# A fused linear-attention and gated-MLP kernel: one x slab at a time in the key loop, two subtractions in halves, and three conversions moved

## The chip, the cores and the metric

The kernel runs on one core of a Trainium2 chip. The metric is the device time of one launch in microseconds; three runs of the kernel before gave 660.51, 662.21 and 662.61, median 662.21. Engines are named as the profile names them: PE is TensorE (matmuls; PEld is its weight load), DVE is VectorE, ACT is ScalarE, POOL is GpSimd, SP is SyncE, which only issues DMAs here. Each engine works through its own instructions in order and waits on semaphores for the others.

## The reference, cut to what matters

With S = 2048 tokens, D = 640, 32 heads of 20 and F = 1536:

```python
xn = layernorm(x)                                   # over D, eps 1e-5
q, k, v = split(xn @ wqkv)                          # 32 heads of 20
pq, pk = q @ w_phi, k @ w_phi                       # per head, 20 x 20
phi_q = concat(softmax(pq), softmax(-pq))           # 40 features a head
phi_k = concat(softmax(pk), softmax(-pk))
kv, z = phi_k.T @ v, phi_k.sum(tokens)
s = ((phi_q @ kv) / (phi_q @ z + 1e-6)) @ wo
g = silu(gelu(xn @ w1 + b1) @ w2 + b2)
out = x + s * g
```

## The kernel before

All matmuls keep fp32 accuracy by splitting each operand into a high part (a rounded copy, made by ScalarE) and a low part (operand minus high part, made by VectorE or GpSimd) and adding three products: high by high, high by low, low by high (PASSES).

**Phase 1** works on 16 tiles of 128 tokens. A key tile takes `project(t, wk_s)` (30 matmuls into one of three PSUM banks, `bankA`), then the features: `feat1` on VectorE (L382 maximum per head, L385 subtract it and write the slab e, L388 minimum), with a last step on GpSimd (L389, below "rest"), `feat2` on ScalarE (L398, exp in place), and `key_fin` (L406 and L438: sums per head and reciprocals on VectorE, L411: scaling on GpSimd). L385 is what frees the bank. `value(t)` is a second projection whose bank ScalarE empties (L427). `kv_pair` adds two tiles into the key-value state. Query tiles take `project`, `feat1` and `store_e`: exp on ScalarE and the store of e to DRAM from ScalarE's queue.

The **normalized and transposed x** is what the projections read as stationary operand. It is held for two tiles together, called a pair q, in the buffers xp (eight blocks, four pairs at a time) and b12 (a slab for two pairs). For q of 4 to 7 these steps make it from x transposed in DRAM:

- `load_xr(q)`: two DMAs on SyncE's queue (L266, L267) into a slab xr
- `pair_stats`: mean and 1/std of two token tiles (L230 to L235 on VectorE, L233 on GpSimd), written to DRAM and read back as rows bc over all partitions (L331, L333)
- `pair_sub(q)`: minus the mean, on GpSimd (L339); `pair_mul(q)`: times 1/std, on VectorE (L344)
- `pair_plain(q)`: high parts on ScalarE (L285, three instructions), low parts on VectorE (L287, three)
- `t_sums(q)`: five differences on GpSimd (L300), in place in xr
- `t_split(q)`: the same split of the differences into the buffer xd: ScalarE (L321) and GpSimd (L322). It is the last reader of the slab xr.

Before xp's blocks of an old pair are written over, `spill(q)` copies them to DRAM (L295, L296, SyncE).

**Slabs.** One pool of 23 buffers of 5 KB a partition (tag "S") holds the split weights (five each for keys, values and queries), b12, xr, every e, and the forms below. A new tile waits for the last user of the buffer that it gets; where none is free, the engine that writes it waits.

The loop over t = 6 to 9 does for each t a key tile, a value tile and two query tiles (of tiles 0 to 7), and beside them pair work. After it, p = 5, 6, 7 take two key tiles each and then `value_pair(p)`: both value tiles of a pair in seven block products instead of eight (`token_pair`, parts X, Y, X, V, Z, W, Z in the order of QPARTS, numbered 0 to 6). It needs five weights split in halves and three sums of weights, S2, S3 (in the slabs f[0] and f[1]), S1 (in the right halves of wv_s[0], wv_s[1]) and S4 (f[2]). `forms` loads the sums and splits them, one group at each `next`. After part 0, ScalarE copies bank X (L654) before part 2 goes on accumulating in it. `hooks` run behind the numbered parts: hook 1 `rest`, hook 4 `first_key` (`key_fin` of the first key tile), hook 6 `second_key`.

From p = 7 on, four token pairs of queries and twelve units of the MLP follow, and the output projection at the end.

All of this part stands under a manual schedule: every engine takes its instructions in the order of the Python text, which is therefore the order in each queue. In the loop that is

```python
es[t] = feat1(pk)
if t > 6: pair_plain(q - 1)          # q = t - 2
if t < 9: pair_sub(q)
if t < 8: load_xr(q + 1)
feat2(es[t]); vs[t] = value(t); phis[t] = key_fin(es.pop(t))
pq = project(next(queries), wq_s); ef = feat1(pq)
if t > 6: t_sums(q - 1)
if t < 9: pair_mul(q)
```

so that slabs of two or three pairs are in use at a time.

Of the kernel before, what the change touches and what calls it, by code (L numbers as in the profile page):

```python
# [8 lines left out]
F32 = mybir.dt.float32  # L9
# [6 lines left out]
P = 128  # L16
# [30 lines left out]
def hedgehog_gated_mlp_kernel(ctx: ExitStack, tc: tile.TileContext, x, xt_in, wqk, bd, wv, wo, w1, b1, w2, b2, out_t):  # L47
# [270 lines left out]
    def t_split(q):  # L318
        dst = xd()[:, :, :, at(q)]
        tt = xrs.pop(q).rearrange("p k (o t) -> p (k o) t", o=2)[:, :9]  # L320
        nc.scalar.activation(dst[:, :, 0, :], tt, AF.Copy)  # L321
        nc.gpsimd.tensor_tensor(dst[:, :, 1, :], tt, dst[:, :, 0, :].bitcast(F32), op=OP.subtract)  # L322

    def pair_stats(t):
        if t % 2 == 0:
# [9 lines left out]
            pld[q] = bc  # L335

    def pair_sub(q):
        bc, xr = pld.pop(q), xrs[q]
        nc.gpsimd.tensor_tensor(xr, xr, bc[:, None, :, 0].to_broadcast([P, KC, W2]), op=OP.subtract)  # L339
        pld[q] = bc  # L340

    def pair_mul(q):
        bc, xr = pld.pop(q), xrs[q]
# [2 lines left out]
    def pair_plain(q):  # L346
        for o in range(2):
            plain(q, o, xrs[q][:, :, o * P:(o + 1) * P])
# [107 lines left out]
    def kv_pair(t):  # L456
        for u in (t, t + 1):
            kv_acc(u, phis.pop(u), vs.pop(u))
# [146 lines left out]
    def split_to(dst, src, eng):  # L605
        nc.scalar.activation(dst[:, 0], src, AF.Copy)
        eng.tensor_tensor(dst[:, 1], src, dst[:, 0].bitcast(F32), op=OP.subtract)

    def forms(dram, f, base, engs):
        raws = [load_raw(dram[k]) for k in range(4)]  # L610
        yield
        for k in range(4):
            if k < 3:
                f.append(slab(F32R, "ws"))
            if k < 2:
                split_to(f[k][:], raws[k][:], engs[k])
            else:
                split_to(base[k - 2][:, :, HALF:], raws[k][:, HALF:], engs[k])
                split_to(f[2][:, :, (k - 2) * HALF:(k - 1) * HALF], raws[k][:, :HALF], engs[k])
            yield  # L620

    QPARTS = (("X", "A11", 0, None), ("Y", "S2", 10, None), ("X", "A12", 2, ("A1k", 4)), ("V", "S3", 12, ("A2k", 7)),
# [73 lines left out]
    x_in(10)  # L696
    x_in(11)
    for t in range(6, 10):
        q = t - 2
        pk = project(t, wk_s)  # L700
        if t == 8:
            kv_pair(6)
        if t == 9:
            vb = forms(sv_dram, wv_f, wv_s, [nc.vector] * 4)
            next(vb)
            w_dump(0)
            w_dump(1)
        if t == 6:
            next(vf[1])
            spill(3)  # L710
        es[t] = feat1(pk)
        if t > 6:
            pair_plain(q - 1)
        if t < 9:
            pair_sub(q)
        if t == 6:
            fold_w(wqT, range(4, KC), "wq", wq_s)
        if t < 8:
            load_xr(q + 1)
        feat2(es[t])  # L720
        vs[t] = value(t)
        phis[t] = key_fin(es.pop(t))
        pq = project(next(queries), wq_s)
        ef = feat1(pq)
        if t > 6:
            t_sums(q - 1)
        if t < 9:
            pair_mul(q)
        for u in STATS.get(t, ()):
            pair_stats(u)  # L730
        store_e(queries_done.pop(0), ef)
        pq = project(next(queries), wq_s)
        ef = feat1(pq)
        if t == 6:
            next(vf[1])
        if t == 9:
            next(vb)
            next(vb)
        if t > 6:
            t_split(q - 1)  # L740
        store_e(queries_done.pop(0), ef)
        if t == 6:
            kv_pair(4)
        for u in XIN.get(t, ()):
            x_in(u)
    qf, later, last_sums = None, [], []
    for p in range(5, 8):
        t = 2 * p
        pk = project(t, wk_s)
        if p == 7:  # L750
            w1r = load_w1(0)
            qf = forms(sq_dram, wq_f, wq_b, [nc.vector, nc.vector, nc.vector, nc.gpsimd])
            next(qf)
        es[t] = feat1(pk)
        if p == 5:
            load_xr(7)
            next(vb)
        if p == 6:
            pair_mul(7)
        pk = project(t + 1, wk_s)  # L760
        kv_pair(t - 2)
        es[t + 1] = feat1(pk, later)
        if p == 7:
            next(qf)
            next(qf)
            q_back(0)
            q_back(1)
            wq_b.extend(wq_s[2:])
        if p == 6:
            pair_plain(7)  # L770

        def rest(t=t, p=p):
            later.pop(0)()
            feat2(es[t])
            if p == 6:
                t_sums(7)
            if p == 7:
                next(qf)

        def first_key(t=t, p=p):  # L780
            phis[t] = key_fin(es.pop(t))
            feat2(es[t + 1])

        def second_key(t=t, p=p):
            if p < 7:
                phis[t + 1] = key_fin(es.pop(t + 1))
            else:
                phis[t + 1] = es.pop(t + 1)
                last_sums.append(key_sums(phis[t + 1]))
            if p == 5:  # L790
                pair_sub(7)
            if p == 6:
                t_split(7)

        value_pair(p, {0: lambda: p == 5 and next(vb), 1: rest, 2: lambda: p == 7 and next(qf), 4: first_key, 6: second_key})
    w1f = w1_forms(w1r)

    def early_rest(q, ea):
# [522 lines left out]
```

## Time and profile before

| | us |
|---|---|
| median of three runs | 662.21 |
| the profiled execution | 661.99 |
| its span in the trace | 660.3 |
| busy: PE, DVE, POOL, ACT | 649.2, 493.0, 399.2, 237.6 |
| granted TensorE clock, mean of the span | 0.996 |

A timeline row gives start, duration, engine, line and operation, output from inputs, shapes, count, and in brackets how long the engine had been idle before it and what ended that. A row with a count covers neighbours that were merged. Matmuls overlap in the array, so the duration of one row of matmuls reaches a little into the next; distances between starts are the better measure. A row of stretches gives the stretch, its length, the busy time and count of each engine, the granted clock (1.00 is full), the DMA engines' busy share and GB/s. The rows themselves are shown where they are used.

### The profile page before, as it was taken

How to read it: one execution, taken by the hardware profiler on the slowest of the kernel's cores; microseconds unless marked ns; L12 is line 12 of the kernel's file. 1: busy time of each engine (PE TensorE's matmuls, PEld its weight loads, DVE VectorE, ACT ScalarE, POOL GpSimd, SP SyncE). 2: the span in 40 equal slices, each digit the busy share in tenths (PEclk: the TensorE clock that was granted, in tenths of full speed). 3: DMA queues.
4: the chain of work that ended last, by engine and by line, in shares of the span. 5: the costliest groups of instructions: out<-in, count | busy, mean ns of one | idle time of the engine just before them, and what ended most of it. 6: DMA issues, size and time to landing. Idle time of an engine off the chain costs nothing.

```text
span 660.3 us, 11417 instructions
## 1 busy us (share of the span) xinstructions
PE 649.2 (98%) x4396; PEld 562.6 (85%) x4396; DVE 493.0 (75%) x739; ACT 237.6 (36%) x345; POOL 399.2 (60%) x357
## 2 busy tenths in 40 slices
PE   9999999989899999999999999999999999999997
PEld 9999999989889998888888888888888887766866
DVE  5785977597887778768979968859789899853232
ACT  3512322324434256252442444841332424132130
POOL 2755476887677854857778876363472967343321
PEclk9999999999999999999999999999999999999999
DMA  9706299427411287527889699787779399999942
GB/s 351 271 1 174 84 336 248 111 94 220 156 42 41 80 258 270 192 85 274 217 263 318 165 406 324 118 308 256 150 213 243 88 268 207 307 256 259 289 165 79
DMA packets 164447, 135.15 MB, mean 205 GB/s; under 512 B 89394, under 2 KB 128562, under 8 KB 164010
## 3 DMA queue, kind: packets, MB, share of 16 engines
q1 hardware_dynamic: 161658, 122.84, 64.0%
q10 hardware_dynamic: 2736, 11.60, 4.9%
q8 instruction: 34, 0.56, 0.4%
q14 instruction: 19, 0.16, 0.1%
HBM read 86.03 MB, written 48.38 MB: 204 GB/s over the span
## 4 chain that ended last, share of the span: by engine, by line
PE 84%; DVE 6%; POOL 5%; ACT 1%; issue 1%; DMA 1%; SPq 0%; ACTq 0%; DVEq 0%; POOLq 0%
PE pB L907 24%; PE pB L878 21%; PE pA L370 14%; PE pB L1065 11%; PE pA L650 5%; PE pA L174 2%; PE pB L1012 2%; POOL e L389 2%; POOL e L411 1%; POOL xr L300 1%; DVE xp L287 1%; PE qV L650 1%; PE kv L450 1%; ACT e L398 1%; DVE rc L406 1%
## 5 line engine op out<-in xcount | busy, mean ns | idle before, releaser
L907 PE MATMUL pB<-hs,w2s 128*128 128x512 f32 x720 | 165.7, 389 | 0.0
L907 PEld LDWEIGHTS pB<-hs,w2s 128*128 128x128 f32 x720 | 135.0, 188 | 28.8 <-DVE y L916 0.8
L878 PE MATMUL pB<-xp,w1s 128*128 128x512 f32 x324 | 81.4, 389 | 0.2 <-DVE pB L1146 0.2
L878 PE MATMUL pB<-xd,w1s 128*128 128x512 f32 x324 | 79.3, 389 | 0.0
L1065 PE MATMUL pB<-oT,wo 128*128 128x512 f32 (+1 forms) x315 | 72.3, 381 | 0.0
L878 PEld LDWEIGHTS pB<-xp,w1s 128*128 128x128 f32 x324 | 60.7, 188 | 13.2 <-DVE pB L1146 0.7
L878 PEld LDWEIGHTS pB<-xd,w1s 128*128 128x128 f32 x324 | 60.8, 188 | 12.6
L411 POOL TENSOR_TENSOR eq<-eq,rc 128x1280 f32<-128x1280 f32 x16 | 37.9, 2369 | 54.7 <-DVE rc L969 36.7
L1065 PEld LDWEIGHTS pB<-oT,wo 128*128 128x128 f32 x315 | 57.2, 188 | 13.8 <-PE pB L1012 2.5
L916 DVE TENSOR_TENSOR y<-pB,y 128x512 f32<-128x512 f32 x100 | 63.1, 675 | 1.4 <-PE pB L907 1.4
L398 ACT ACTIVATE e<-e 128x1280 f32<-128x1280 f32 x32 | 40.7, 1273 | 60.7 <-POOL e L389 60.7
L389 POOL TENSOR_TENSOR e<-nr,e 128x640 f32<-128x640 f32 x32 | 46.7, 1460 | 22.6 <-DVE nr L388 20.3
L883 ACT ACTIVATE pB<-pB,b1t 128x512 f32<-128x512 f32 x48 | 31.8, 662 | 78.8 <-DVE pB L1146 29.2
L411 POOL TENSOR_TENSOR e<-e,rc 128x1280 f32<-128x1280 f32 x16 | 39.2, 2450 | 34.5 <-DVE rc L438 34.5
L370 PE MATMUL pA<-wk,xp 128*128 128x320 f32 x384 | 59.6, 310 | 0.0
L370 PEld LDWEIGHTS pA<-wk,xp 128*128 128x128 f32 x384 | 56.9, 188 | 0.1
L956 POOL TENSOR_TENSOR ez<-eq,zrep 128x1280 f32<-128x1280 f32 x16 | 47.4, 2961 | 2.6 <-DMA eq<-e_dram 2.6
L478 POOL TENSOR_TENSOR w1s<-raw,w1s 128x640 fp32r<-128x640 f32 (+1 forms) x18 | 25.0, 1391 | 29.4 <-ACT w1s L477 23.3
L370 PE MATMUL pA<-wv,xp 128*128 128x320 f32 x240 | 37.7, 311 | 0.0
L1068 POOL TENSOR_TENSOR xres<-gt,xres 128x256 f32<-128x256 f32 x20 | 14.3, 735 | 35.3 <-DVE gt L1067 35.3
L370 PEld LDWEIGHTS pA<-wv,xp 128*128 128x128 f32 x240 | 35.5, 188 | 0.1
L889 DVE TENSOR_TENSOR hs<-pB,hs 128x512 fp32r<-128x512 f32 x48 | 32.0, 683 | 3.8 <-ACT hs L885 3.6
(182 smaller groups left out, 1148.8 us busy)
## 6 DMA issues: line engine op xcount, KB each, us to landing
raw<-in_w_dram SPq DMA_DIRECT2D x42, 320.0 KB
e_dram<-e ACTq DMA_DIRECT2D x16, 640.0 KB
eq<-e_dram SPq DMA_DIRECT2D x16, 640.0 KB
phi_t<-eq SPq DMA_DIRECT2D x64, 160.0 KB
phT<-phi_t SPq DMA_DIRECT2D x20, 480.0 KB
xt<-in_x_dram SPq DMA_DIRECT2D x16, 320.0 KB
xres<-in_xt_dram SPq DMA_DIRECT2D x20, 256.0 KB
out_dram<-xres SPq DMA_DIRECT2D x18, 256.0 KB
```

Source lines behind the costliest of these rows:

```text
L370: nc.tensor.matmul(ps[:, hf, :HALF], stat_x(q, o, k, a), ws[k][:, b, hf * HALF:(hf + 1) * HALF], start=n == 0, stop=n == 3 * KC - 1)
L389: rest = lambda: nc.gpsimd.tensor_tensor(e5[:, :, :, 1, :], nr[:, :, :, None].to_broadcast([P, 2, 16, DH]), e5[:, :, :, 0, :], op=OP.subtract)
L398: nc.scalar.activation(ef, ef, AF.Exp)
L411: nc.gpsimd.tensor_tensor(e3, e3, rc[:, :, None].to_broadcast([P, 64, DH]), op=OP.mult)
L650: nc.tensor.matmul(bank[ch], q_x(blk, a, q), p_weight(base, f, w, k)[:, b], start=ch not in seen and n == 0, stop=n == len(mms) - 1, skip_ ...
L878: nc.tensor.matmul(bank[ch][:], tl[:, a, off + wo_:off + wo_ + P], mov(blk, b), start=new and n == 0, stop=n == len(mms) - 1, skip_group_c ...
L883: nc.scalar.activation(ps, ps, AF.Gelu_apprx_tanh, bias=b1t[:, f:f + 1])
L889: nc.vector.tensor_tensor(hs[:, 1], ps, hs[:, 0].bitcast(F32), op=OP.subtract)
L907: nc.tensor.matmul(ps[:], ws[i][:, b, d * P:(d + 1) * P], hs[o][i][:, a, :], start=i == n == 0, stop=(i, n) == (GF - 1, 2), skip_group_che ...
L916: nc.vector.tensor_tensor(y, ps[:], y, op=OP.add)
L956: nc.gpsimd.tensor_tensor(zv, ef, zf, op=OP.mult)
L1065: nc.tensor.matmul(ps[:, mv], w, o[:, mv], start=n == 0, stop=n == 15, skip_group_check=True)
```

## The change

- `pair_sub` becomes two instructions, one for each half of the pair's 256 tokens; the GpSimd part of `t_split` becomes two, of five and four blocks. The rows bc stay in `pld` until `pair_mul` takes them.
- In the loop, q is t - 3, and for t of 7 to 9 the tile does mul, plain and sums of pair q behind the exp of its key tile, the split behind the first query's features, and then the load of the next xr. For t of 7 and 8 the subtraction of pair q + 1 comes behind the second query's features. Tile 6 keeps only `pair_sub(4)`; `load_xr(5)` and (6) move one tile on, `load_xr(7)` moves from p = 5 to t = 9.
- `spill(3)` moves from t = 6 to t = 8.
- `forms` gets `s4_last` for the value sums: the third `next` (p = 5, behind the first key tile's features) splits both halves of S1; the copies of S4 come at hook 1 and its low parts at hook 4. Before, S1 and S4 were split half by half, at the third `next` and at hook 0.
- `pair_sub(7)` moves from hook 6 of p = 5 to hook 3, `pair_mul(7)` from p = 6 to hook 6 of p = 5, `pair_plain(7)` of p = 6 ahead of the second key projection.

```diff
     def t_split(q):
         nc.scalar.activation(dst[:, :, 0, :], tt, AF.Copy)
-        nc.gpsimd.tensor_tensor(dst[:, :, 1, :], tt, dst[:, :, 0, :].bitcast(F32), op=OP.subtract)
+        for o in (slice(0, 5), slice(5, 9)):
+            nc.gpsimd.tensor_tensor(dst[:, o, 1, :], tt[:, o], dst[:, o, 0, :].bitcast(F32), op=OP.subtract)
...
     def pair_sub(q):
-        bc, xr = pld.pop(q), xrs[q]
-        nc.gpsimd.tensor_tensor(xr, xr, bc[:, None, :, 0].to_broadcast([P, KC, W2]), op=OP.subtract)
-        pld[q] = bc
+        bc, xr = pld[q], xrs[q]
+        for o in (slice(0, P), slice(P, W2)):
+            nc.gpsimd.tensor_tensor(xr[:, :, o], xr[:, :, o], bc[:, None, o, 0].to_broadcast([P, KC, P]),
+                                    op=OP.subtract)
...
-    def forms(dram, f, base, engs):
+    def forms(dram, f, base, engs, s4_last=False):
...
                 split_to(base[k - 2][:, :, HALF:], raws[k][:, HALF:], engs[k])
-                split_to(f[2][:, :, (k - 2) * HALF:(k - 1) * HALF], raws[k][:, :HALF], engs[k])
+            if k == 2 and s4_last:
+                continue
+            parts = [(f[2][:, :, (j - 2) * HALF:(j - 1) * HALF], raws[j][:, :HALF], engs[j])
+                     for j in ((2, 3) if s4_last and k == 3 else (k,) if k >= 2 else ())]
+            if s4_last and k == 3:
+                yield
+            for d, r, _ in parts:
+                nc.scalar.activation(d[:, 0], r, AF.Copy)
+            if s4_last and k == 3:
+                yield
+            for d, r, eng in parts:
+                eng.tensor_tensor(d[:, 1], r, d[:, 0].bitcast(F32), op=OP.subtract)
             yield
...
     for t in range(6, 10):
-        q = t - 2
+        q = t - 3
         pk = project(t, wk_s)
         if t == 8:
             kv_pair(6)
+            spill(3)
         if t == 9:
-            vb = forms(sv_dram, wv_f, wv_s, [nc.vector] * 4)
+            vb = forms(sv_dram, wv_f, wv_s, [nc.vector] * 4, True)
...
-            spill(3)
         es[t] = feat1(pk)
         if t > 6:
-            pair_plain(q - 1)
-        if t < 9:
-            pair_sub(q)
-        if t == 6:
+            feat2(es[t])
+            pair_mul(q)
+            pair_plain(q)
+            t_sums(q)
+        else:
+            pair_sub(4)
             fold_w(wqT, range(4, KC), "wq", wq_s)
-        if t < 8:
-            load_xr(q + 1)
-        feat2(es[t])
+            feat2(es[t])
         vs[t] = value(t)
         phis[t] = key_fin(es.pop(t))
         pq = project(next(queries), wq_s)
         ef = feat1(pq)
         if t > 6:
-            t_sums(q - 1)
-        if t < 9:
-            pair_mul(q)
+            t_split(q)
+            load_xr(q + 1)
         for u in STATS.get(t, ()):
             pair_stats(u)
         store_e(queries_done.pop(0), ef)
...
-        if t > 6:
-            t_split(q - 1)
+        if t in (7, 8):
+            pair_sub(q + 1)
         store_e(queries_done.pop(0), ef)
...
         if p == 5:
-            load_xr(7)
             next(vb)
         if p == 6:
-            pair_mul(7)
+            pair_plain(7)
         pk = project(t + 1, wk_s)
...
-        if p == 6:
-            pair_plain(7)
 
         def rest(t=t, p=p):
+            if p == 5:
+                next(vb)
             later.pop(0)()
...
         def first_key(t=t, p=p):
+            if p == 5:
+                next(vb)
             phis[t] = key_fin(es.pop(t))
...
             if p == 5:
-                pair_sub(7)
+                pair_mul(7)
             if p == 6:
                 t_split(7)
 
-        value_pair(p, {0: lambda: p == 5 and next(vb), 1: rest, 2: lambda: p == 7 and next(qf), 4: first_key, 6: second_key})
+        value_pair(p, {1: rest, 2: lambda: p == 7 and next(qf), 3: lambda: p == 5 and pair_sub(7), 4: first_key, 6: second_key})
```

## The prediction

> **What bounds the kernel now.** I read the page's totals first, then the busy time of chosen stretches, then the timelines of TensorE, VectorE, GpSimd, ScalarE and SyncE over 95 to 200 us.
>
> ```profile
> span 660.3 us, 11417 instructions
> PE 649.2 (98%) x4396; PEld 562.6 (85%) x4396; DVE 493.0 (75%) x739; ACT 237.6 (36%) x345; POOL 399.2 (60%) x357
> ```
>
> TensorE is the bound (98%), so only its waits can be won. Next the stretches: length, then busy us and count of PE, PEld, DVE, ACT, POOL, then granted clock, DMA share, GB/s.
>
> ```profile
> 134.63:156.57 21.94, 19.60 (x122) 19.13 (x121) 18.93 (x28) 7.04 (x8) 16.11 (x17) 0.92 0.34 84
> 166.79:177.74 10.95, 8.83 (x61) 8.04 (x55) 9.74 (x13) 6.01 (x10) 6.21 (x8) 1.00 0.41 133
> 187.96:197.75 9.79, 8.55 (x61) 8.02 (x55) 9.58 (x11) 4.98 (x8) 6.22 (x7) 1.00 0.26 71
> 207.94:215.98 8.04, 8.04 (x63) 8.04 (x55) 6.62 (x10) 4.96 (x9) 4.14 (x4) 1.00 0.01 3
> 146.80:150.20 3.40, 3.40 (x16) 3.40 (x16) 2.45 (x4) 2.20 (x2) 3.40 (x4) 0.58 0.07 5
> ```
>
> The first four are key 9, value 9, the queries of that tile, and then the value pairs p=5, 6 and 7. Pair 7 runs without a wait in 8.04 us; pair 5 takes 2.9 us more, pair 6 1.75 more. In the fifth the clock is 0.58.
>
> ```profile
> 97.62 2.02 PE L370 MATMUL pA<-wk,b 128*128 128x320 f32 x12
> 115.33 4.56 PE L370 MATMUL pA<-wk,xp 128*128 128x320 f32 x30
> 139.68 1.99 PE L370 MATMUL pA<-wv,b 128*128 128x320 f32 x12 [0.48 <-DVE e L385]
> 146.17 6.17 PE L370 MATMUL pA<-wq,xp 128*128 128x320 f32 x30 [1.86 <-DVE e L385]
> 152.17 1.92 PE L370 MATMUL pA<-wq,b 128*128 128x320 f32 x12
> 173.84 1.89 PE L650 MATMUL pA<-wv,xd 128*128 128x320 f32 x11 [1.02 <-DVE wv L607]
> 190.94 1.58 PE L650 MATMUL pA<-wv,xp 128*128 128x320 f32 x9 [0.95 <-ACT qx L654]
> 197.75 4.56 PE L370 MATMUL pA<-wk,xp 128*128 128x320 f32 x30
> ```
>
> The four projections of tile 7 fill 97.62 to 115.33: 4.43 us each. Four of tile 9's take 21.94, so it loses 21.94 - 4 x 4.43 = 4.2 us; 1.6 of them are the slow clock (146.17 to 152.17 is 6.0 us). Lost in all: 4.2 + 2.9 + 1.75 = 8.9 us, the most that the change can win.
>
> ```profile
> 114.90 1.49 DVE L344 TENSOR_TENSOR xr<-xr,bc 128x1280 f32<-128x1280 f32 x1 [0.34 <-DMA xt<-in_x_dram]
> 116.31 0.88 DVE L230 BATCH_NORM_STATS2 st<-xt 128x6 f32<-128x320 f32 x2
> 118.88 0.82 DVE L382 TENSOR_REDUCE mx<-pA 128x32 f32<-128x640 f32 x1
> 124.79 0.82 DVE L385 TENSOR_TENSOR e<-pA,mx 128x640 f32<-128x640 f32 x1 [5.09 <-DMA e_dram<-e]
> 132.55 3.46 DVE L287 TENSOR_TENSOR xp<-xr,xp 128x384 fp32r<-128x384 f32 x1
> 135.94 1.47 DVE L406 TENSOR_REDUCE rc<-e 128x64 f32<-128x1280 f32 x1
> 137.91 0.76 DVE L382 TENSOR_REDUCE mx<-pA 128x32 f32<-128x640 f32 x1
> 144.35 0.81 DVE L382 TENSOR_REDUCE mx<-pA 128x32 f32<-128x640 f32 x1
> 146.79 0.81 DVE L382 TENSOR_REDUCE mx<-pA 128x32 f32<-128x640 f32 x1
> 186.51 2.56 DVE L344 TENSOR_TENSOR xr<-xr,bc 128x1280 f32<-128x1280 f32 x1 [1.63 <-POOL xr L339]
> ```
>
> The root is the row at 124.79: VectorE has a query's e to write and waits 5.09 us for the store of the query before, which still holds its slab. All 23 slabs are taken: 15 weights, two b12, xr4, xr5, xr6, e of tiles 6 and 7, that query's e. VectorE stays late, and the banks that tile 9 wants are read late (L385 is named at 139.68 and 146.17). Pair 6 waits because pair_mul(7) at 186.51 waited for pair_sub(7), which stood behind two key scalings.
>
> **The change part by part.** Tiles 7 to 9 now take pair q through mul, plain, sums and split within the tile, and the next load comes behind the split. At the stall's place the count is one or two lower (xr4, and xr5 if it is loaded early), so a slab is free and the 5.09 us go. No arithmetic is removed. For the rest I walked the new order through the queues: each engine in program order, each instruction when its inputs are there, at these prices.
>
> ```profile
> 111.87 3.00 POOL L339 TENSOR_TENSOR xr<-xr,bc 128x1280 f32<-128x1280 f32 x1 [3.82 <-DMA bc<-st_dram]
> 132.31 3.28 POOL L339 TENSOR_TENSOR xr<-xr,bc 128x1280 f32<-128x1280 f32 x1
> 140.53 2.46 POOL L389 TENSOR_TENSOR e<-nr,e 128x640 f32<-128x640 f32 x1
> 142.96 3.57 POOL L300 TENSOR_TENSOR xr<-xr 128x256 f32<-128x256 f32 x5
> 148.75 2.69 POOL L322 TENSOR_TENSOR xd<-xr,xd 128x1152 fp32r<-128x1152 f32 x1
> 156.84 2.37 POOL L411 TENSOR_TENSOR e<-e,rc 128x1280 f32<-128x1280 f32 x1 [3.43 <-DVE rc L438]
> 159.16 1.28 POOL L389 TENSOR_TENSOR e<-nr,e 128x640 f32<-128x640 f32 x1
> 183.43 3.05 POOL L339 TENSOR_TENSOR xr<-xr,bc 128x1280 f32<-128x1280 f32 x1
> ```
>
> ```profile
> 127.91 1.28 ACT L398 ACTIVATE e<-e 128x1280 f32<-128x1280 f32 x1 [3.28 <-POOL e L389]
> 129.59 0.74 ACT L285 ACTIVATE xp<-xr 128x640 fp32r<-128x640 f32 x1 [0.40 <-ACT e L398]
> 133.56 0.68 ACT L427 ACTIVATE v<-pA 128x640 f32<-128x640 f32 x1
> ```
>
> VectorE: feat1 2.44 (144.35 to 146.79), statistics 2.57 (116.31 to 118.88), head sums and reciprocal 1.97 (135.94 to 137.91), pair_mul 1.49. GpSimd: rest 1.28, sums 3.57, scaling 2.37. ScalarE: exp 1.28, plain's three copies 1.4 (0.74 for 640 of 1280 columns), value copy 0.68. The trace has no split half. Five sums cover the 1152 columns of one t_split and take 0.88 us more, 0.22 for each further instruction; so a cut costs 0 to 0.22, and I take 0.2, since that row is such a cut: pair_sub 2 x 1.62, t_split 2.9. A rule of overlap comes from two pairs of rows: the GpSimd op at 132.31 ends at 135.6 and VectorE's of 132.55 ends 0.4 later, so it waited the other out; rest took 2.46 beside pair_mul in place of 1.28. So in the walk a GpSimd op and a VectorE op with two SBUF inputs exclude each other. The same walk in the order of before, its slab stall put in, ends pair 6 at 196.2, and 197.8 with the slow clock's 1.6; the row says 197.75.
>
> Tile 6: pair_mul(4) leaves, query 1's feat1 is 1.4 us earlier, and GpSimd is through v_forms at 105.0.
>
> Tile 7: feat1 ends 104.7; rest and pair_mul(4) collide, rest is done at 107.5, exp 108.8, plain's copies 110.1, its VectorE parts 111.7, the key's sums 113.7, query 116.2, statistics 118.7, query 121.2, key 8 123.7. GpSimd: sums 111.4, scaling 116.2, rest 117.6, split 120.4, powers 121.5, rest 122.7, pair_sub(5) 125.9, rest of key 8 127.2.
>
> Tile 8: pair_mul(5) waits for pair_sub(5); exp is done at 128.5, plain 131.9, the queries 136.4 and 141.4, key 9 143.8; GpSimd is last again, pair_sub(6) at 146.1, rest 147.3. Tile 9: exp 148.6, plain's copies 150.2, value copy 150.8, queries 156.5 and 159.0, split 160.7.
>
> TensorE, unhindered, starts key 9 at 134.4, value 9 at 138.8, the queries at 143.2 and 147.7, keys 10 and 11 at 152.1 and 156.5. Each wants the bank of the projection three before: free at 130.6 (value copy 8), 135.5, 140.5, 143.0, 150.8 (value copy 9), 155.6. All are in time, the closest by 0.9. So tile 9's 4.2 us go. What hides GpSimd's longer tile (20.1 us from rest of key 8 to rest of key 9, TensorE's 19.0 with its key-value sums) is the lead of three banks; without it 1 us a tile would show.
>
> Pair 5 starts at 162.3. S1 is now converted ahead of it, S4 within. The exp of query 7 ends at 163.7, two S1 copies and the copy of X follow to 165.2, where part three wants it at 164.0: 1.2 lost. VectorE is through feat1 of tile 11 at 169.9 and the pair's two sums at 170.9; S4's parts then alternate with rest(11) and the first half of pair_sub(7): done 171.6 and 173.4, while TensorE came to them at 170.1. That loses 1.55 and 1.35; uncut, pair_sub(7) would hold the second 1.6 longer. So pair 5 loses 4.1 in place of 2.9. Pair 6: pair_sub(7) ends 174.8, pair_mul(7) 179.5, plain's copies 181.0, ahead of the copy of X at 185.5. Its 1.75 go.
>
> SyncE: an xr load now stands behind the tile before's statistics and x loads and, at tile 8, behind spill(3).
>
> ```profile
> 92.42 5.91 SPq L296 DMA_DIRECT2D xp_dram<-b  x1
> 100.79 1.00 SPq L331 DMA_DIRECT2D st_dram<-pst  x1
> 107.78 0.34 SPq L333 DMA_DIRECT2D bc<-st_dram  x1
> 111.34 0.44 SPq L266 DMA_DIRECT2D xr<-in_xt_dram  x1
> ```
>
> At tile 8 the x loads are out at about 129, spill's issue takes up to 6.3, so load_xr(6) goes at 135 and lands near 140 (a load issued at 107.78 was used at 111.87, 4.1 us); pair_sub(6) wants it at 142.8. If that cover of 3 us goes, each us late is a us of GpSimd. Load_xr(5) goes at about 109, as soon as a slab is free.
>
> The sum: won 8.9, lost again 1.2 + 1.55 + 1.35 = 4.1, net 4.8. Pair 7 and all behind it wait on nothing of theirs, so it stays to the end. The profiled execution took 661.99 (span 660.3), 0.2 below the median of 662.21: 662.2 - 4.8 = 657.4.
>
> Bounds: with cuts at nothing, the walk loses 0.8 less, 656.6. If the exclusion of the two engines didn't hold, nothing is lost: 653.3. If GpSimd is 2 us later a tile than walked, value copy 9 and the bank of query 6 cost 2 to 4: 661.
>
> **Rivals.** First, the slow clock again: before, 2.1 us of idle (to 146.17) came ahead of 3.4 us of it, and pair 5 will idle 2.9 of 3.3 us. By that row 1.6 come back: 659.0. Against it: 1.0 us waits (173.84, 190.94) cost no clock.
>
> [...]
>
> Second, at tile 9 the forms S2 and S3 want two slabs at 159.5, where 13 weights, two b12, xr6, xr7, e8, e9, two query e and both forms make 23. If the first waits for query 6's store (issued 159.1, 3 to 5 us by what the 5.09 row leaves), it starts at 162 to 164: 1.3 to 3.3 us more, 658.7 to 660.7.
>
> Third, the other side: load_xr(q+1) gets the very slab that t_split(q) frees. Then pair_sub waits from the split's end (120.4, 140.6) for issue and landing. The load issued at 107.78 follows a write of 100.79 that took 7.0 to land. At 5.5 us key 10 waits 4.8 us for value copy 9 and the walk ends 6.8 later, 664.2, with the slow clock 665.8; at 7.0, 667.2. It decides from 4.5 us on. For it: the order keeps one x slab. Against it: load_xr(6) went out at 111.34 with one slab left, so a load takes any.
>
> Fourth, the pool stays full at tile 7, as xr5 comes early and another tile takes the slab won: the 5.09 us stay, 5.1 more by the walk, 662.5.
>
> **How the numbers follow.** Forecast 0.56, clock 0.14, forms 0.10, pool full 0.08, load behind the split 0.12. This kernel's measurement can tell about 0.3%, 2.0 us. Faster (below 660.2): the first two and over half of the third, 0.76; same 0.12 (the rest of it, the full pool); slower 0.12, the load. The range leaves out the slower case, the full pool and the end without exclusion: 653.8 to 661.8.
>
> **What would show it.** After: no wait of VectorE for a store of e near 119; tile 9's projections back to back at clock 1.00; S4's parts and pair_sub(7) alternating near 171, with TensorE waiting there; no wait in pair 6. It is wrong if key 10 waits for a value copy, pair_sub(5) or (6) for a DMA, a form for a slab.

## Result and profile after

The changed kernel took 657.97 us, the median of six executions (656.97 to 660.41), beside 662.11 for six of the kernel before (660.51 to 662.61) on the same chip: ratio 0.9946, 95% interval 0.9925 to 0.9967. The forecast was 657.4. The profiled execution is the slowest of the six, 660.41 with a span of 658.7; its mean clock, 0.995, is the lowest of the six (the others 0.996 to 1.000), which is seen below.

The stretches of the kernel after (length, busy us and count of PE, PEld, DVE, ACT, POOL, then granted clock, DMA share, GB/s) for tile 9, the value pairs 5, 6 and 7, and the key projection between pairs 5 and 6:

```profile
134.50:156.50 22.00, 22.00 (x153) 22.00 (x152) 18.07 (x29) 8.22 (x9) 18.59 (x21) 1.00 0.75 226
162.31:175.79 13.48, 9.79 (x62) 8.72 (x55) 12.93 (x15) 6.34 (x10) 8.02 (x10) 0.92 0.32 106
188.12:196.14 8.02, 8.02 (x61) 8.02 (x55) 4.80 (x8) 3.64 (x5) 5.21 (x7) 1.00 0.16 45
206.34:214.37 8.03, 8.03 (x61) 8.03 (x55) 6.60 (x10) 4.96 (x9) 4.14 (x4) 1.00 0.02 5
175.79:182.30 6.51, 6.51 (x32) 6.51 (x31) 4.46 (x6) 1.46 (x3) 5.58 (x2) 0.64 0.40 115
```

Tile 9 is busy without a gap, pair 6 is as short as pair 7, and pair 5 has become longer: 13.48 us where it was 10.95. The last row is one projection, which takes 4.40 us at clock 1.00 (152.10 to 156.50) and 6.51 here, at 0.64. TensorE's timeline of the kernel after:

```profile
152.10 4.56 PE L372 MATMUL pA<-wk,xp 128*128 128x320 f32 x30
165.94 1.58 PE L663 MATMUL pA<-wv,xp 128*128 128x320 f32 x9 [1.61 <-ACT qx L667]
171.81 0.42 PE L663 MATMUL pA<-ws,xp 128*128 128x320 f32 x1 [0.72 <-DVE v L677]
172.51 0.70 PE L663 MATMUL pA<-ws,xp 128*128 128x320 f32 x3 [0.29 <-DVE ws L632]
174.29 0.90 PE L663 MATMUL pA<-ws,xp 128*128 128x320 f32 x2 [1.08 <-DVE ws L632]
175.79 6.67 PE L372 MATMUL pA<-wk,xp 128*128 128x320 f32 x30
196.14 4.56 PE L372 MATMUL pA<-wk,xp 128*128 128x320 f32 x30
```

Only pair 5 waits: for the copy of X (1.61), a value sum (0.72) and S4's low parts (0.29 and 1.08). The first projection behind pair 6 starts at 196.14, where it was 197.75: 1.61 us, and the two profiled executions differ by 661.99 - 660.41 = 1.58. GpSimd, then VectorE, kernel after:

```profile
110.61 3.93 POOL L300 TENSOR_TENSOR xr<-xr 128x256 f32<-128x256 f32 x5 [2.87 <-DVE xp L287]
114.62 2.38 POOL L413 TENSOR_TENSOR e<-e,rc 128x1280 f32<-128x1280 f32 x1
118.18 2.82 POOL L323 TENSOR_TENSOR xd<-xr,xd 128x640 fp32r<-128x640 f32 x2
123.22 3.15 POOL L341 TENSOR_TENSOR xr<-xr,bc 128x640 f32<-128x640 f32 x2
143.30 3.15 POOL L341 TENSOR_TENSOR xr<-xr,bc 128x640 f32<-128x640 f32 x2
172.07 3.60 POOL L341 TENSOR_TENSOR xr<-xr,bc 128x640 f32<-128x640 f32 x2
```

```profile
119.59 0.82 DVE L387 TENSOR_TENSOR e<-pA,mx 128x640 f32<-128x640 f32 x1
171.66 2.58 DVE L632 TENSOR_TENSOR ws<-raw,ws 128x320 fp32r<-128x320 f32 x2
178.86 1.43 DVE L346 TENSOR_TENSOR xr<-xr,bc 128x1280 f32<-128x1280 f32 x1
```

The query's e that waited 5.09 us for a slab is written at 119.59 without a wait. The low parts (171.66 to 174.24) and pair_sub(7) (172.07 to 175.67) run through each other, and pair_mul(7) at 178.86 waits for nothing.

### The profile page after: what moved, and what is told of

It is laid out like the page before. It is cut to its first block, busy times and chain, and to the rows that moved or that the text cites. A ratio compares the mean times of both kernels' runs of the same rounds, so it can differ in the third digit from the quotient of the medians.

```text
span 658.7 us, 11422 instructions
## 1 busy us (share of the span) xinstructions
PE 649.6 (99%) x4396; PEld 563.9 (86%) x4396; DVE 488.3 (74%) x739; ACT 237.6 (36%) x345; POOL 396.8 (60%) x366
## 4 chain that ended last, share of the span: by engine, by line
PE 78%; DVE 8%; POOL 6%; DMA 3%; issue 2%; SPq 1%; ACT 1%; ACTq 0%; DVEq 0%; POOLq 0%
PE pB L920 24%; PE pB L891 21%; PE pB L1078 11%; PE pA L372 9%; PE pA L663 6%; PE pB L1025 2%; DMA st_dram<-pst 2%; POOL xr L341 1%; POOL xd L323 1%; POOL e L391 1%; PE qV L663 1%; POOL xr L300 1%; PE pA L174 1%; DVE xr L346 1%; DMA xt<-in_x_dram 1%
## 5 line engine op out<-in xcount | busy, mean ns | idle before, releaser
L372 PE MATMUL pA<-wk,xp 128*128 128x320 f32 x384 | 61.7, 317 | 0.0
L391 POOL TENSOR_TENSOR e<-nr,e 128x640 f32<-128x640 f32 x32 | 43.8, 1368 | 26.1 <-DVE nr L390 23.7
L372 PEld LDWEIGHTS pA<-wk,xp 128*128 128x128 f32 x384 | 59.1, 195 | 0.1
```

Of the source, the lines that this page charges most:

```text
L372: nc.tensor.matmul(ps[:, hf, :HALF], stat_x(q, o, k, a), ws[k][:, b, hf * HALF:(hf + 1) * HALF], start=n == 0, stop=n == 3 * KC - 1)
L391: rest = lambda: nc.gpsimd.tensor_tensor(e5[:, :, :, 1, :], nr[:, :, :, None].to_broadcast([P, 2, 16, DH]), e5[:, :, :, 0, :], op=OP.subtract)
```

## Experiments

One number stands for the change in a profiled execution: the start of the first projection behind pair 6. From there to the end of the span all fourteen kernels take 462.5 to 462.6 us (before 660.3 - 197.75, after 658.7 - 196.14), so nothing behind it moves. Ahead of the waits in question the profiled executions already differ by up to 0.8 us (tile 7's first projection starts at 97.19 to 97.96), so smaller differences of this mark say nothing. The times are medians, each ratio is to the kernel before on the same chip.

| kernel | us | ratio, 95% interval | pair 5 | pair 6 | behind pair 6 |
|---|---|---|---|---|---|
| before | 662.11 | 1 | 10.95 | 9.79 | 197.75 |
| after | 657.97 | 0.9946 (0.9925 to 0.9967) | 13.48 | 8.02 | 196.14 |
| e1_spill_alone | 657.83 | 0.9944 (0.9927 to 0.9961) | 11.54 | 9.80 | 193.73 |
| e2_load6_late | 663.00 | 1.0015 (1.0005 to 1.0026) | 10.67 | 9.74 | 199.04 |
| e3_pair7_alone | 660.15 | 0.9977 (0.9961 to 0.9993) | 12.16 | 8.01 | 195.82 |
| e4_uncut | 659.89 | 0.9976 (0.9963 to 0.9990) | 13.87 | 8.03 | 194.92 |
| e5_spill_at_6 | 657.97 | 0.9947 (0.9931 to 0.9963) | 12.64 | 8.02 | 192.85 |
| e6_spill_and_pair7 | 655.97 | 0.9919 (0.9903 to 0.9936) | 11.41 | 8.02 | 191.99 |
| e7_sub7_at_9 | 656.31 | 0.9923 (0.9907 to 0.9940) | 11.62 | 8.03 | 192.14 |
| e8_22_slabs | 658.40 | 0.9955 (0.9940 to 0.9971) | 13.44 | 8.02 | 194.13 |
| e9_split6_later | 657.55 | 0.9949 (0.9933 to 0.9966) | 13.14 | 8.03 | 193.29 |
| e10_lows_earlier | 656.90 | 0.9933 (0.9914 to 0.9953) | 12.32 | 8.02 | 192.64 |
| e11_sub7_hook5 | 655.98 | 0.9917 (0.9902 to 0.9932) | 9.49 | 10.08 | 191.71 |
| e12_sub7_hook1 | 654.92 | 0.9900 (0.9883 to 0.9917) | 10.12 | 8.02 | 190.93 |

The stretches are those of one execution each. In the kernel after, e3, e4, e8 and e10 some of a low clock lies inside pair 5, in the others none; so 13.48 us is best set beside the 12.64 of e5, which has the same steps there.

The theory that went into them (A): TensorE's waits in three places are separate accounts. Tile 9's come from the late slab and its chain, pair 6's from pair 7's steps, pair 5's from the order of VectorE and GpSimd there. The rivals are named with each.

**e1_spill_alone.** The kernel before with one line moved:

```diff
         if t == 8:
             kv_pair(6)
+            spill(3)
...
             next(vf[1])
-            spill(3)
```

> The kernel before with one edit: spill(3) at t = 8 in place of t = 6. Theory A (the loss begins where VectorE waits 5.09 us at 118.9 for a slab, and anything that ends that wait sooner wins it back): without spill(3)'s 1.3 MB ahead of it on the queue the rows bc(5) come some 4 us sooner, pair_sub(5) doesn't wait 3.8 us on GpSimd at 108 to 112, the query's store goes out near 117.5 in place of 121.2, the wait for the slab shrinks from 5.09 to about 1.3 us and tile 9's 4.2 us go: 657.5 to 658.5, pair 6's waits stay. Rival B (only the new order of the steps within a tile, which holds one x slab, removes it): 661 to 662, the wait of 5 us stays.

657.83: this line alone brings what the whole change brings. Timelines of SyncE, ScalarE's queue, GpSimd and VectorE in this kernel:

```profile
99.03 0.37 SPq L331 DMA_DIRECT2D st_dram<-pst  x1
103.56 0.34 SPq L333 DMA_DIRECT2D bc<-st_dram  x1
118.36 0.33 ACTq L682 DMA_DIRECT2D e_dram<-e  x1
107.94 3.32 POOL L339 TENSOR_TENSOR xr<-xr,bc 128x1280 f32<-128x1280 f32 x1
121.86 0.82 DVE L385 TENSOR_TENSOR e<-pA,mx 128x640 f32<-128x640 f32 x1 [2.67 <-ACT xd L321]
```

Before, spill(3) held SyncE's queue for 5.91 us at 92.42, ahead of the statistics' round trip; bc went out at 107.78 and pair_sub(5) waited for it until 111.87. Without it bc goes at 103.56 and the subtraction starts at 107.94, 3.9 us earlier, with no wait. Of the 4.2 us by which bc is earlier, 1.8 are the earlier issue of the write ahead of it (99.03 against 100.79) and 2.5 its shorter way (4.5 us to bc's issue against 7.0), which the spill's traffic may account for; no run separates the two. The slab wait is not gone: it is 2.67 in place of 5.09. The row names the ScalarE half of t_split(4), but GpSimd's half still reads xr4 until 127.60, so this is not the slab that came free. The query's store fits: it goes out at 118.36 in place of 121.20, and VectorE writes 3.50 us after its issue, where it was 3.59. Tile 9 runs without a wait all the same, so it absorbs 2.67 us.

**e2_load6_late.** The kernel before with load_xr(6) moved behind the second query's features of tile 7, so that a slab is free at 119:

```diff
-        if t < 8:
+        if t == 6:
             load_xr(q + 1)
...
             t_split(q - 1)
+        if t == 7:
+            load_xr(q + 1)
```

> The kernel before with one edit: load_xr(6) behind the second query's features of tile 7, so that one slab more is free at 118.9. Theory A: the wait of 5.09 us is gone, though bc(5) is as late as before; tile 9's 4.2 us go, pairs 5 and 6 keep theirs: 657.5 to 658.5. Rival C (the wait is the lateness of the transfers behind spill(3), a slab more changes nothing): 661 to 662.

663.0, and the forecast of A is missed. The slab wait is gone, but other losses stand in its place (VectorE, SyncE, GpSimd, TensorE):

```profile
114.59 5.69 DVE L344 TENSOR_TENSOR xr<-xr,bc 128x1280 f32<-128x1280 f32 x1 [0.70 <-POOL xr L339]
129.17 0.76 SPq L266 DMA_DIRECT2D xr<-in_xt_dram  x1
136.21 3.05 POOL L339 TENSOR_TENSOR xr<-xr,bc 128x1280 f32<-128x1280 f32 x1 [5.02 <-DMA xr<-in_xt_dram]
156.54 6.21 PE L370 MATMUL pA<-wk,xp 128*128 128x320 f32 x30 [2.40 <-ACT v L427]
```

VectorE loses ahead of the query's e what it wins there: pair_mul(5), 1.49 us in the kernel before, takes 5.69 beside GpSimd's scaling and rest, and e is written at 123.62, where it was 124.79. The load that went out at 111.34 now goes at 129.17, behind the round trip of tile 7's statistics, and lands 7.0 us later; GpSimd stands 5.02 us for it, and key 10 waits 2.40 for value copy 9. Those are the place, the landing time and the sign of the prediction's third rival, which foresaw 4.8 us for that wait. The experiment doesn't show what the slab wait alone costs, since it puts a longer pair_mul and a late load in its place.

**e3_pair7_alone.** The kernel before with pair 7's steps where the change has them, and nothing else:

```diff
         if p == 6:
-            pair_mul(7)
+            pair_plain(7)
         pk = project(t + 1, wk_s)
...
             if p == 5:
-                pair_sub(7)
+                pair_mul(7)
...
-        value_pair(p, {0: lambda: p == 5 and next(vb), 1: rest, 2: lambda: p == 7 and next(qf), 4: first_key, 6: second_key})
+        value_pair(p, {0: lambda: p == 5 and next(vb), 1: rest, 3: lambda: p == 5 and pair_sub(7), 2: lambda: p == 7 and next(qf), 4: first_key, 6: second_key})
```

> The kernel before with only the steps of the last pair moved: pair_sub(7) to hook 3 and pair_mul(7) to hook 6 of p = 5, pair_plain(7) ahead of the second key projection of p = 6; load_xr(7) and all else stay. Theory A: pair 6 loses nothing (1.75 us before), tile 9 and pair 5 lose as before or up to 1 us more in pair 5, where pair_sub(7) now meets the low parts: 660.3 to 661.5. Rival (pair 6's wait comes from the lateness of tile 9 and not from the place of pair_sub(7)): 662, pair 6 still at 9.8 us.

660.15, just below A's range. Pair 6 takes 8.01 us, and tile 9 keeps its waits (1.86 us at 146.03) with the slab's at full length (VectorE, TensorE):

```profile
124.66 0.82 DVE L385 TENSOR_TENSOR e<-pA,mx 128x640 f32<-128x640 f32 x1 [5.06 <-DMA e_dram<-e]
169.20 2.63 PE L650 MATMUL pA<-wv,xp 128*128 128x320 f32 x9 [1.75 <-ACT qx L654]
```

**e4_uncut.** The changed kernel with pair_sub and t_split whole again:

```diff
-        for o in (slice(0, 5), slice(5, 9)):
-            nc.gpsimd.tensor_tensor(dst[:, o, 1, :], tt[:, o], dst[:, o, 0, :].bitcast(F32), op=OP.subtract)
+        nc.gpsimd.tensor_tensor(dst[:, :, 1, :], tt, dst[:, :, 0, :].bitcast(F32), op=OP.subtract)
...
-        for o in (slice(0, P), slice(P, W2)):
-            nc.gpsimd.tensor_tensor(xr[:, :, o], xr[:, :, o], bc[:, None, o, 0].to_broadcast([P, KC, P]),
-                                    op=OP.subtract)
+        nc.gpsimd.tensor_tensor(xr, xr, bc[:, None, :, 0].to_broadcast([P, KC, W2]), op=OP.subtract)
```

> The changed kernel with pair_sub and t_split uncut. Theory A: the cuts cost 0.2 us each (tiles 7 to 9 get 0.4 us a tile back on GpSimd), but the second low part of S4 waits for 3.05 us of pair_sub(7) in place of 1.6: pair 5 some 1.0 to 1.4 us longer, 658.5 to 659.5. Rival (the shorter holds are what wins in tiles 7 to 9): tile 9 waits again, 660 to 662.

659.89, a little above A's range; tile 9 has no waits. In pair 5 (GpSimd, VectorE, TensorE):

```profile
170.70 3.19 POOL L339 TENSOR_TENSOR xr<-xr,bc 128x1280 f32<-128x1280 f32 x1
170.29 3.94 DVE L629 TENSOR_TENSOR ws<-raw,ws 128x320 fp32r<-128x320 f32 x2
164.56 1.58 PE L660 MATMUL pA<-wv,xp 128*128 128x320 f32 x9 [0.70 <-ACT qx L664]
174.29 0.81 PE L660 MATMUL pA<-ws,xp 128*128 128x320 f32 x2 [2.44 <-DVE ws L629]
```

VectorE's second low part is done only at 174.23, 0.3 us behind the end of GpSimd's instruction (173.89); the two low parts take 3.94 us, against 2.58 where the subtraction is cut. With the subtraction in halves (kernel after) they are done at 174.24, 1.43 us ahead of its end (175.67); in e9, where it ends 3.3 us before they start, they take 0.95.

The cut wins 1.36 us there (2.44 - 1.08), but it also costs: uncut, the wait for the copy of X is 0.70, 0.91 less than in the changed kernel, and GpSimd's tile is 0.3 us shorter (from the sums of tile 8 to those of tile 9 19.83 us against 20.13). Together the waits of pair 5 are only 0.45 longer in e4. The medians lie 1.9 us apart; the rest of that was not taken apart, but all twelve executions of e4 lost some of the clock, and three of six of the changed kernel (the last section).

**e5_spill_at_6.** The changed kernel with the spill back at tile 6:

```diff
         if t == 8:
             kv_pair(6)
-            spill(3)
...
             next(vf[1])
+            spill(3)
         es[t] = feat1(pk)
```

> The changed kernel with spill(3) back at tile 6, so the new order without the moved spill. Theory A (either half of the change removes the late slab: with one slab fewer alive, the early spill delays nothing that VectorE needs): no waits of TensorE over 0.3 us in tile 9, 657 to 659.5, ratio 0.992 to 0.997. Rival B (the moved spill carries the whole gain and the new order adds nothing by itself): the waits of tile 9 return, 661 to 663, ratio 0.998 to 1.002.

657.97, the same as with the spill moved, and no wait in tile 9 (SyncE, GpSimd):

```profile
91.47 5.79 SPq L296 DMA_DIRECT2D xp_dram<-b  x1
105.07 0.33 SPq L334 DMA_DIRECT2D bc<-st_dram  x1
122.66 3.20 POOL L341 TENSOR_TENSOR xr<-xr,bc 128x640 f32<-128x640 f32 x2
```

The spill is ahead of the round trip again. It makes bc(5) only 0.9 us later than in the changed kernel (104.19), since load_xr(5), which stood between the two before, has moved as well; and the new order asks for bc(5) only at 122.66, 17.6 us after its issue. So for tile 9 the moved spill and the new order are two cures of one illness, and each is enough; their gains don't add.

**e6_spill_and_pair7.** The edits of e1 and e3 together.

> The kernel before with the moved spill and pair 7's steps moved one place later, and nothing else of the change. Theory A (the two gains lie in different stages and add up: 4.2 to 4.5 us of tile 9, 1.7 to 2.0 us of pair 6): 655.5 to 657.0, ratio 0.990 to 0.993, below the changed kernel. Rival B (they overlap: what one wins is lost again in pair 5, as the changed kernel did): 657.5 to 658.5, ratio 0.9935 to 0.995, level with the changed kernel.

655.97. The gains of e1 (661.84 - 657.83 = 4.0) and e3 (1.7) add up to 5.7, and 661.63 - 655.97 is 5.7. This leaves out the new order of tiles 7 to 9, the cuts and the moved S4, and its median is 2.0 us below the changed kernel's (ratios 0.9919 and 0.9946; all five executions are below the fastest of that); pair 5 takes 11.41 us in it, against 13.48, or 12.64 at full clock in e5. What the moved S4 does to pair 5 by itself no run shows.

**e7_sub7_at_9.** The changed kernel with pair_sub(7) out of pair 5:

```diff
-        if t in (7, 8):
+        if t > 6:
             pair_sub(q + 1)
...
-        value_pair(p, {1: rest, 2: lambda: p == 7 and next(qf), 3: lambda: p == 5 and pair_sub(7), 4: first_key, 6: second_key})
+        value_pair(p, {1: rest, 2: lambda: p == 7 and next(qf), 4: first_key, 6: second_key})
```

> The changed kernel with pair_sub(7) issued at the end of tile 9 instead of in pair 5. Theory A (the two waits on S4's low parts in pair 5, 1.37 us together, come from pair_sub(7) and rest(11) in front of them; one of the two is left): pair 5 loses 2 to 3 us instead of 3.7, 656.3 to 657.3, ratio 0.991 to 0.993. Rival B (GpSimd then waits for the load of xr(7) with pair 5's e tiles queued behind it): new waits on e in pair 5, 658.5 to 661, ratio 0.994 to 0.999.

656.31, at the edge of A's range. The wait of 1.08 us on S4's second low part is gone, the other three stay (1.39, 0.70, 0.29).

**e8_22_slabs.** The changed kernel with `bufs=22` in the pool of slabs.

> The changed kernel with 22 slabs instead of 23. Theory A (the change holds one slab less in tiles 6 to 9, but stages before and after still need 23): somewhere a wait for a slab returns, 658.5 to 662, ratio 0.995 to 1.000, with a VectorE or DMA wait on a slab of 1 us or more. Rival B (22 are now enough everywhere): no new wait, 656.9 to 658.2, ratio as the changed kernel's 0.9925 to 0.994.

658.4, between the two ranges. A wait for a slab is back (VectorE), smaller than before and without cost in tile 9:

```profile
120.97 0.82 DVE L387 TENSOR_TENSOR e<-pA,mx 128x640 f32<-128x640 f32 x1 [1.48 <-POOL xd L323]
```

So the change does fill all 23 slabs near 120, and one fewer costs 0.4 us, which these runs can't tell from none.

**e9_split6_later.** e7 with t_split(6) behind the second query's e, to hasten the exp ahead of the copy of X:

```diff
-            t_split(q)
+            if t < 9:
+                t_split(q)
             load_xr(q + 1)
...
+        if t == 9:
+            t_split(q)
         if t > 6:
             pair_sub(q + 1)
```

> e7_sub7_at_9 with one more step moved: t_split(6) of tile 9 behind the second query's e instead of ahead of it, so ScalarE reaches the copy of X some 2 us earlier. Theory A (VectorE's unbroken row from 160.7 to 172 sets the end of pair 5, and the wait on the copy of X lies beside it): the 1.39 us wait goes or shrinks below 0.4 and the waits on v and the low parts grow by as much; pair 5 still loses 2.0 to 2.6 us, time 656.0 to 656.7. Rival B (GpSimd's order sets the end of pair 5): the 1.39 us are won, 654.5 to 655.2.

657.55: worse than either theory; the wait for the copy of X is 1.69 us in place of 1.39. GpSimd and TensorE:

```profile
162.99 2.79 POOL L323 TENSOR_TENSOR xd<-xr,xd 128x640 fp32r<-128x640 f32 x2 [2.46 <-ACT xd L321]
169.34 1.26 POOL L391 TENSOR_TENSOR e<-nr,e 128x640 f32<-128x640 f32 x1
172.29 1.60 PE L663 MATMUL pA<-wv,xd 128*128 128x320 f32 x9 [2.89 <-ACT v L672]
```

The split has a ScalarE half (at 161.70), and this moved too, behind the copies of the forms; GpSimd stood 2.46 us for it, and its row behind it (split, pair_sub(7), e of key 10) ends at 170.60, 2.7 us later than in e7. The copy of the first value half waits in ScalarE's queue behind that e's exp.

**e10_lows_earlier.** e9 with ScalarE's copies for the first two forms ahead of the first query's exp; VectorE's low parts of them, which are the same instructions, come at two later `next`:

```diff
+        if s4_last:
+            for k in range(2):
+                f.append(slab(F32R, "ws"))
+                nc.scalar.activation(f[k][:][:, 0], raws[k][:], AF.Copy)
+            yield
...
             if t < 9:
                 t_split(q)
+            else:
+                next(vb)
```

> e9_split6_later with ScalarE's two copies for the forms of tile 9 ahead of the exp of the first query, so VectorE's low parts (two of 0.91 us that waited 2.1 us for them) can start at 158.7 and all of VectorE's row in pair 5 comes up to 2 us earlier. Theory A (VectorE's row sets the end of pair 5): pair 5 loses 1 us or less, 654.0 to 655.2. Rival B (another engine is next: GpSimd's subtraction for pair 7 ahead of key 10's e): pair 5 still loses 1.5 us or more, 655.5 to 656.7.

656.9, with one wait of 2.75 us left in pair 5 (VectorE, GpSimd, ScalarE, TensorE):

```profile
158.41 2.63 DVE L623 TENSOR_TENSOR ws<-raw,ws 128x640 fp32r<-128x640 f32 x2
163.84 3.62 POOL L341 TENSOR_TENSOR xr<-xr,bc 128x640 f32<-128x640 f32 x2
167.42 1.27 POOL L391 TENSOR_TENSOR e<-nr,e 128x640 f32<-128x640 f32 x1
169.90 0.42 ACT L679 ACTIVATE v<-pA 128x320 f32<-128x320 f32 x1
170.37 2.77 PE L670 MATMUL pA<-wv,xd 128*128 128x320 f32 x9 [2.75 <-ACT v L679]
```

The low parts start at 158.41, and the wait on the copy of X is gone. Rival B's mechanism holds: pair_sub(7) stands ahead of key 10's e (167.42), whose exp stands on ScalarE ahead of the copy of the first value half (169.90), for which TensorE waits. The time is 0.2 above B's range; four of the six executions lost some of the clock.

**e11_sub7_hook5** and **e12_sub7_hook1.** e10 with pair_sub(7) at two other places:

```diff
-        if t > 6:
+        if t in (7, 8):
             pair_sub(q + 1)
...
-        value_pair(p, {1: rest, 2: lambda: p == 7 and next(qf), 4: first_key, 6: second_key})
+        value_pair(p, {1: rest, 2: lambda: p == 7 and next(qf), 4: first_key, 5: lambda: p == 5 and pair_sub(7), 6: second_key})
```

> e10_lows_earlier with pair_sub(7), 3.6 us on GpSimd, taken out from ahead of key 10's e and put behind key 10's sums in pair 5. Theory A (the one wait left, 2.75 us for the copy of the first value half, is the exp of key 10 waiting for an e that GpSimd writes only after pair_sub(7): 167.4 instead of 163.9): no wait over 0.6 us in pair 5, 653.3 to 654.8 where the clock stays at 1.0. Rival B (VectorE's row sets the end of pair 5 all the same): waits of 1.5 us or more on v or the low parts, 655.0 to 656.5.

```diff
             if p == 5:
                 next(vb)
+                pair_sub(7)
             later.pop(0)()
```

> e10_lows_earlier with pair_sub(7) between key 10's e and key 11's e on GpSimd, where VectorE then works on the low parts. [...] Rival B (the place in pair 5 does not matter once key 10's e goes first): level with e11_sub7_hook5 within 0.3 us.

e11 took 655.98, outside A's range, and e12 654.92, which had been estimated at 654.3 to 655.8, above e11. The order of the two is the other way round, and at 1.06 us apart they are not level either, though the waits of pair 5 have the size that was expected: 0.49 us at most in e11, 1.32 together in e12. e11 (GpSimd, VectorE, TensorE):

```profile
174.94 3.13 POOL L341 TENSOR_TENSOR xr<-xr,bc 128x640 f32<-128x640 f32 x2
178.10 3.64 DVE L346 TENSOR_TENSOR xr<-xr,bc 128x1280 f32<-128x1280 f32 x1 [2.92 <-POOL xr L341]
169.43 0.42 PE L670 MATMUL pA<-ws,xp 128*128 128x320 f32 x1 [0.49 <-DVE v L684]
190.29 1.14 PE L670 MATMUL pA<-ws,xp 128*128 128x320 f32 x6 [0.97 <-DVE v L684]
```

Pair 5 takes 9.49 us, but the subtraction at 174.94 makes pair_mul(7) wait 2.92 us and then run into the key scaling, 3.64 in place of 1.43; key 12's features stand behind it on VectorE, and pair 6 takes 10.08. What pair 5 won is given back there. e12 (the same engines):

```profile
166.83 3.14 POOL L341 TENSOR_TENSOR xr<-xr,bc 128x640 f32<-128x640 f32 x2
169.55 2.26 DVE L639 TENSOR_TENSOR ws<-raw,ws 128x320 fp32r<-128x320 f32 x2
171.86 0.56 PE L670 MATMUL pA<-ws,xp 128*128 128x320 f32 x2 [0.78 <-DVE ws L639]
```

The subtraction (to 169.97) runs beside VectorE's features of key 11, three instructions of 0.81 to 0.82 us from 166.05 to 168.65, of which the first two read TensorE's bank. They are as long in e11, where GpSimd stands idle beside the last two (166.61 to 168.46). The subtraction meets the low parts (from 169.55) only at its end. Pair 5 waits 1.32 us in all, pair 6 not at all. This is the fastest of the fourteen: 3.05 us below the changed kernel (ratios 0.9900 and 0.9946).

## Why the prediction was right, step by step

- **Tile 9's 4.2 us go: right.** The four projections of tile 9 take 152.10 - 134.50 = 17.6 us, 4.40 each, at clock 1.00. The walk had key 9 at 134.4 and key 10 at 152.1; they start at 134.50 and 152.10. pair_sub(5) and (6), walked to 125.9 and 146.1, end at 126.4 and 146.5.
- **"The root is the row at 124.79": half of it.** e1 shows what is ahead of it: the spill on SyncE's queue, bc 4.2 us later, GpSimd 3.9 us later, the query's store 2.8 us later. A slab wait of 2.67 us costs tile 9 nothing. The prediction priced the moved spill only as a risk for load_xr(6); it had not seen that by itself it wins the same 4 us.
- **The cuts: nearly right.** Taken at 0.2 us each; pair_sub takes 3.15 beside the whole one's 3.05, t_split 2.82 beside 2.69, and GpSimd's tile with both is 0.3 longer than in e4, so 0.1 to 0.15. The bound "with cuts at nothing, the walk loses 0.8 less" has its counterpart in e4's 0.91 at the copy of X. What they win, "uncut, pair_sub(7) would hold the second 1.6 longer", is 2.44 - 1.08 = 1.36 in e4.
- **A dependency was left out.** The sums write xr in place and so wait for plain's low parts: they end at 114.54 where the walk had 111.4. The scaling behind them, which waited for its reciprocal anyway, starts at 114.62; the walk had it end at 116.2, it ended at 117.0.
- **Pair 5's loss: right in place, short in size.** Forecast 1.2 at the copy of X and 1.55 + 1.35 at S4's low parts, 4.1 us; measured waits 1.61, then 0.72 + 0.29 + 1.08, together 3.70, and the stretch is 13.48 - 8.03 = 5.45 longer than pair 7. The walk had no term for what is left. e5 has the same four waits, 3.52 us together, at full clock through pair 5, and loses 12.64 - 8.03 = 4.61, 1.1 us more than its waits; e12 with three waits loses 0.77 more than they are long (10.12 - 8.03 - 1.32). The other 0.7 us of the changed kernel's 5.45 go with the clock at the end of the stretch (0.92 in its mean).
- **Pair 6's 1.75 go: right,** and e3 shows that pair 7's steps do it alone.
- **The slow clock (14%) came true in half of the executions.** Three had a mean clock of 0.999 or 1.000 and took 656.97 to 657.48, around the forecast without it; three had 0.995 to 0.997 and took 658.45 to 660.41, around the rival's 659.0. So the median lies 0.6 us above the forecast, and the profiled execution 3.0. With three of each kind the median is the middle between 657.48 and 658.45, and that it falls so near the forecast is in part luck. The idle time ahead of the drop before was 1.86 us by the row at 146.17, not 2.1, and that drop, counted whole among the 8.9 us to be won, is not in every execution: of 58 executions of the kernel before that ran beside the experiments, 33 had a mean clock of 0.997 or less.
- **The other rivals fell.** No form waited for a slab. The pool is full, but nothing that sets the end stands for it (e8). load_xr(6) went out at 133.6 behind the spill and was there in time.
- **The net of 4.8 us** was 4.1 in the medians. In the two profiled executions key 10 starts 156.57 - 152.10 = 4.47 earlier, pair 5 takes 13.48 - 10.95 = 2.53 longer, the projections behind it 12.33 - 10.22 = 2.11 longer (the clock), and pair 6 9.79 - 8.02 = 1.77 less: 1.60 net, as the marks behind pair 6 have it.

## What to carry to other kernels

Price a moved transfer by what stands behind it on the issuing queue, not only by what it carries: one spill ahead of a round trip of statistics was worth as much as a reordered tile. When two parts of a change cure the same wait, their gains don't add; try each alone before paying for both, here for the second's harm in pair 5. The same long instruction of GpSimd cost more or less by what VectorE did beside it: pair_sub(7) in halves took 3.14 us beside key 11's features, which stayed at 0.81 to 0.82 each (e12; 3.13 in e11, where VectorE waited for it), and 3.60 beside S4's low parts, which took 2.58 (kernel after) and 0.95 without it (e9). Cutting it cost 0.1 to 0.15 us here and brought those low parts to 2.58 us from 3.94 (e4). Add the cuts up where they stand ahead of something tight: together they cost 0.9 us at the copy of X here.

## What was not expected of the hardware

In these runs a lower clock goes along with waits of TensorE of 1.61 to 2.89 us, and not in every execution. In e1, e7, e11 and e12, whose longest wait between tile 9 and pair 6 is 1.09, 1.39, 0.97 and 0.78 us in the profiled execution, none of 20 executions had a mean clock below 0.999. In the kernel after, e8, e3, e2, e4, e10 and e9, which have waits of 1.61, 1.62, 1.86, 2.40, 2.44, 2.75 and 2.89, 39 of 59 had 0.997 or less: all 12 of e4, but 2 of 5 of e9. The grouping was made behind the fact, and no run varies a wait alone. In e8 the matmuls right behind a wait of 1.62 us are slow, nine in 2.39 us, where the kernel after took 1.58 for the same nine (165.94):

```profile
166.71 2.39 PE L663 MATMUL pA<-wv,xp 128*128 128x320 f32 x9 [1.62 <-ACT qx L667]
```

The traces show where the low clock lies. Ahead of the kernel's end, the kernel before has one stretch of it, 3.41 us at clock 0.50 (146.27 to 149.68), and the kernel after one of 6.83 (173.64 to 180.47). The full clock that the trace records ahead of it and behind it lasts 139.95 us (from 6.32) and 508.59 (to 658.27) before, 167.25 (from 6.39) and 477.87 (to 658.34) after, which is 41, 149, 49 and 140 times 3.413 us. Stretches of this length around the low clock (columns as above), two of the kernel before, four of the kernel after, the last of them double, and two of e10:

```profile
142.85:146.27 3.42, 1.56 (x11) 1.33 (x11) 3.25 (x11) 1.27 (x1) 3.19 (x6) 1.00 0.34 142
146.27:149.68 3.41, 3.41 (x14) 3.41 (x15) 2.98 (x4) 2.03 (x2) 3.41 (x5) 0.50 0.19 55
163.40:166.82 3.42, 1.81 (x13) 1.55 (x12) 3.21 (x6) 3.02 (x7) 0.39 (x1) 1.00 0.46 192
166.82:170.23 3.41, 3.41 (x25) 3.36 (x24) 3.20 (x4) 1.71 (x3) 2.10 (x6) 1.00 0.12 22
170.23:173.64 3.41, 1.98 (x10) 1.23 (x9) 3.31 (x5) 1.27 (x1) 2.80 (x2) 1.00 0.29 90
173.64:180.47 6.83, 6.17 (x23) 6.18 (x24) 6.58 (x8) 0.15 (x1) 5.78 (x4) 0.50 0.46 138
166.43:169.85 3.42, 1.19 (x9) 0.92 (x7) 2.04 (x4) 1.13 (x1) 3.42 (x8) 1.00 0.00 0
169.85:173.26 3.41, 2.89 (x11) 2.89 (x12) 3.27 (x6) 1.74 (x3) 1.13 (x1) 0.50 0.53 149
```

TensorE idled 1.86, 1.43 and 2.23 us in the stretch ahead of these three drops. Idle time of that length is not enough by itself: 1.61 us of it, from 163.40 on in the kernel after, has clock 1.00 behind it. And e9, with the longest wait of all, keeps clock 1.00 in the two stretches that hold it, with 1.50 and 1.39 us of idle time:

```profile
167.49:170.90 3.41, 1.91 (x14) 1.65 (x12) 2.82 (x4) 0.26 (x1) 3.41 (x8) 1.00 0.00 0
170.90:174.31 3.41, 2.02 (x13) 2.02 (x14) 2.50 (x5) 2.61 (x3) 2.00 (x2) 1.00 0.34 101
```

That it matters where a wait falls among such stretches is the author's reading of these rows; no run tests it.

If the drop comes from the wait, which no run shows either, removing the wait is worth more than its length: at tile 9 of the kernel before 1.6 of the 4.2 us lost were the clock.
